# Reordering four kinds of helper work in a fused kernel: windowed attention and two feed-forward networks on one core

## The chip, the cores and the metric

The kernel runs on one core of one Trainium2 chip. A core has five engines with a queue each: TensorE (PE in the rows, its weight loads PEld), VectorE (DVE), ScalarE (ACT), GpSimd (POOL), and SyncE (SP), which here only issues transfers. Each engine works through its own instructions in the order in which they stand in its queue, and waits on semaphores for the others. The metric is the device time of one execution in microseconds (us), taken as the median of several executions; less is better.

## The reference

Attention over 4 batches, 8 heads, 576 positions and 64 channels, in which each query sees at most 32 keys (heads 0 to 3: the last 32 positions; heads 4 to 7: every fourth of the last 128); then two feed-forward networks of 2304 tokens, width 512, inner width 2048, one behind the other.

```python
scores = scale * np.matmul(q, k.transpose(0, 1, 3, 2))
scores = np.where(masks[None, :, :, :], scores, -1000000000.0)
attn = np.exp(scores - np.max(scores, axis=-1, keepdims=True))
attn_out = np.matmul(attn / (np.sum(attn, axis=-1, keepdims=True) + 1e-09), v)
x = np.ascontiguousarray(attn_out.transpose(0, 2, 1, 3)).reshape(B * S, H * D)
# network 1
h = x @ w_in
x = (np.maximum(h, 0.0) + alpha * np.minimum(h, 0.0)) @ w_out
# network 2
h = x @ w_in2
out = np.where(h >= 1, h, np.where(h <= -1, 0.0, (h + 1) ** 2 / 4.0)) @ w_out2
```

## The kernel before

**Split products.** Every large product is made of three matmuls in a reduced 32-bit format: each factor is split into a high part (a rounding copy on ACT, line 326) and a low part (source minus high part on POOL or DVE, line 327). For weights the parts are `wr` (of w_in) and `woh`, `wol` (of w_out); for the activations `xv` (input x) and `gh`, `gl` (the inner activation g). Lines 513 to 515 are the three matmuls of h = x w_in in the plain sub-tiles, lines 688 to 690 those of y = g w_out.

**Conversions.** The weights arrive as 64-bit words in staging tiles `st` (line 271, one transfer of 512 KB on SP's queue each) and are turned into 32-bit numbers by three DVE instructions: lines 320, 321 and 314. `conv(k)` issues the next k of these instructions. When the third is issued the staging tile is free and the next load is issued (`more`). Lists hold what is still to load (`pend_l`) and to convert (`pend_w`); the second network's 16 w_in tiles stand in `pend_2`. A conversion of the second network's w_in goes by `wf` to DRAM.

**Stages.** (1) Six attention groups alone. (2) The sub-tiles `PLAIN` = (0,0), (0,1), (0,2) of network 1, each in 16 slots f, one for every 128 inner columns; a counter k runs over the slots. A slot issues on PE the products h(f), an attention step and y(f-2); on the other engines the activation (`f_g`: line 650 on ACT, 653 on DVE, 660 on ACT for `gh`), the low part `gl` (`f_cut`, line 666), splits of weights and conversions. Twelve groups of attention run inside these slots, at the slots' two attention points: scores `s_ps` (line 148), their maximum and difference on DVE (155, 160), exp on ACT (164), a transpose on PE to `t_ps` (211), its copy to `pT` on ACT (213), the values' product `o_ps` (222), its scaling on DVE (228 to 230), a transpose to `x_ps` (237) and copies into x (255). (3) `PAIRS`, (0,3), (1,0) and (1,1): sub-tiles of 1024 tokens by a seven-product scheme (lines 544 to 546), whose combined inputs are sums made on DVE in PSUM (`room`, line 452) and then split into `xv`. Between two pairs stands a loop over `SECOND`, 16 steps of 12 matmuls each (the second half's y), in which the next pair's weights (`p_weights`) and inputs (`x_work`, 22 pieces of work, handed out by `more_x`) are prepared. (4) `LAST`.

**What sets the order.** The order on every engine is the order of the calls in the code; nothing is rescheduled. In slots 0 and 1 the products h(0) and h(1) have been issued already, so both slots run as fast as the other engines allow. `h_ps` has two PSUM tiles, so h(2) waits for line 653 of slot 0, which reads h(0). In network 1's first sub-tile `gl` is on POOL.

**The lines that the change touches.** `w_cut` splits the w_in tiles whose conversion is finished; `split_pending` splits the w_out tiles whose y is still to come; `EARLY` gives the number of conversion instructions in slots 0 and 1, `BEFORE` how many of a slot's stand between the parts of the activation.

Of the kernel before, what the change touches and what calls it, by code (L numbers as in the profile page):

```python
# [26 lines left out]
NF = DFF // P  # L27
# [29 lines left out]

FIRST = (0, 2)

EARLY = (3, 6)  # L60
READY = 12
BEFORE = ((1, 1), (1, 3))

# [4 lines left out]
PLAIN = ((0, 0), (0, 1), (0, 2))  # L68
# [19 lines left out]
def attention_then_two_ffns(ctx: ExitStack, tc: tile.TileContext, a0, aqk, av, w1i, w1o, w2i, w2o, alpha, masks, ident, out):  # L88
# [170 lines left out]
    wi, wo, wt, cv, cut = {}, {}, {}, {}, []  # L259
# [107 lines left out]
    def w_cut():  # L367
        while cut:
            w_split(*cut.pop(0))
# [335 lines left out]
    def pieces(ph):  # L705

        return [(ph, 0, 0), (ph, 1, 0)] + [x for f in range(NF) for x in ((ph, f + 2, 0), (ph, f, 1)) if x[1] < NF]
# [4 lines left out]
    with tc.manual_schedule(), ExitStack() as late:  # L712
# [19 lines left out]
        pend_l = pieces(0)  # L732
# [36 lines left out]
        def conv(k):  # L769

            for _ in range(k):
                if not todo and pend_w and pend_w[0] in cv:
                    todo.extend(w_make(*pend_w.pop(0)))
                if todo:
                    todo.pop(0)()
                    if not todo:
                        more()
# [47 lines left out]
        f_h(n0, 1, (2,))  # L825
        x_split(n0, 3)
        w_cut()
        conv(3)
        nc.vector.tensor_scalar(al, al, -1.0, 1.0, ALU.mult, ALU.add)
        a_load_qk(NGB + 1)  # L830
        a_load_v(NGB + 1)
# [45 lines left out]
        def more_x(k):  # L877
            for _ in range(min(k, len(x_work))):
                x_work.pop(0)()
# [7 lines left out]
        def split_pending():  # L887
            for x in pend_y:
                if x not in wos:
                    wo_split(*x)  # L890

        def one_y():
            f_y(*pend_y.pop(0))

        pend_2 = [(1, f, 0) for f in range(NF)]
        after_n = dict(zip(order, order[1:] + [None]))

        def slot(n, f, k):
            nn = after_n[n]
            if k != 1:  # L900
                split_pending()
            w_cut()
            if n == LAST and f == NF - 1:
                wo_split((n, 0), f)
            if k > 1 or n == LAST:
                f_h(n, f)
            early = f < 2 and k > 1
            if early:
                one_y()
            if n == PLAIN[0] and f == NF - 1:  # L910
                pend_l.extend(pend_2)
                pend_w.extend(pend_2)
            if n in PLAIN[:2] and f >= NF - NC:
                x_split(nn, f - NF + NC, n == PLAIN[1])
            if k in (0, 1):
                ops = EARLY[k]
            elif n == n0:
                ops = 6
            elif n != LAST:
                ops = 1 if n == PLAIN[1] else 3  # L920
            else:
                ops = 0
            attention_point()
            b0, b1 = BEFORE[n[0]]
            g = f_g(n, f, lambda: conv(min(ops, b0)))
            ops -= min(ops, b0)
            first_ops = min(ops, b1) if k else 1
            conv(first_ops)
            f_cut(n, f, g)
            if k == 0:  # L930
                wo_split((n, 0), f)
            w_cut()
            ahead = 2 if n == PLAIN[0] else 3
            for i in range(1, ahead + 1):
                if f + i < NF:
                    ready(n, f + i)
                elif nn and nn not in PAIRS:
                    ready(nn, f + i - NF)
            if n == PLAIN[2]:
                if f == 9:  # L940
                    turn = iter(range(1 << 30))
                    x_work.extend(x_seven(nn, lambda: ps_a.tile([P, TW], F32, tag="w" if nxt < NG or at else "wa"[next(turn) % 2], name="room")))
                if NF - 4 <= f < NF - 1:
                    p_weights(nn, 0, f - NF + 4)
                if f in (9, 10):
                    more_x(3)
                elif f >= READY:
                    more_x((5, 5, 6, len(x_work))[f - READY])
                if f == NF - 1:
                    p_weights(nn, 0, 3)  # L950
                if f == NF - 1:
                    r_free.extend(x_free[:2])
                    del x_free[:2]
            if n == LAST and f % 2 == 0 and 4 <= f // 2 + 3 < NF // 2:
                w_base(1, f // 2 + 3)
            if k >= 2 and not early:
                one_y()
            pend_y.append(((n, 0), f))
            attention_point()
            conv(ops - first_ops)  # L960
            more()

        k = 0
# [53 lines left out]
        for q, n in enumerate(PAIRS):  # L1017
# [41 lines left out]
            for i, f in enumerate(SECOND):  # L1059
                if i and loaded < NF:  # L1060
                    g_load(n, SECOND[loaded])
                    loaded += 1
                if 1 <= i < NF - 2:
                    wo_split((n, 1), SECOND[i + 2])
                if i == NF - 2:
                    more_x(len(x_work))
                    if nn in PAIRS:
                        step(q + 1, 0)
                    else:
                        pend_y += [((n, 1), x) for x in SECOND[i:]]  # L1070
                        break
                f_y((n, 1), f)
                more_x(2)
                if nn in PAIRS:
                    if i in (5, 13):
                        w_base(nn[0], i // 13)
                    if i == NF - 3:
                        r_free.extend(x_free[:2])
                        del x_free[:2]
                    elif i in (8, 9, 10, 11):  # L1080
                        p_weights(nn, 0, i - 8)
                else:
                    if i == 0:
                        r_free.extend(x_free[:8])
                        del x_free[:8]
                    if i % 4 == 0:
                        w_base(nn[0], i // 4)
                    elif i % 2 == 0:
                        ready(nn, i // 2 - 1)
                    if i % 4 == 0 and i:  # L1090
                        ready(nn, i // 2 - 1)
                if q == 0:
                    for _ in range((2, 1, 1, 0, 0, 1, 1, 1, 1)[i] if i < 9 else 0):
                        w_load(*pend_l.pop(0))
                    if i == 8:
                        spare += [0, 0]
                    if f in HELD:
                        wo[1, f] = w_pool(f).tile([P, DM], F32, tag=f"o{f}", name="wo")
                        nc.sync.dma_start(wo[1, f], whole[1, 1, f // 2][:, f % 2])
                    if i < NF - 1 and SECOND[i + 1] not in HELD:  # L1100
                        conv(3)
                    if i == NF - 4:
                        assert not pend_w and not todo and not cv
                        x_free.extend(st_free)
                        st_free.clear()
# [91 lines left out]
```

## Time and profile before

| what | value |
|---|---|
| median of 3 runs | 860.86 us (858.82 to 861.88) |
| the profiled execution: its time | 859.94 us |
| the profiled execution: span from first to last instruction | 858.2 us |
| mean granted clock of TensorE | 0.992 of 2.4 GHz |
| busy share of the span: PE, PEld, DVE, ACT, POOL | 98%, 80%, 65%, 50%, 56% |

The profiled execution lasts 1.7 us longer than its span, and it lies 0.92 us under the median. PE is the engine that sets the time, so a change of order can only win where PE stands still or runs at the lower clock. The rows further down are in the trace's form: start in us from the span's start, length in us, engine, line, operation, tile written <- tiles read, shapes, how many instructions the row holds, and in brackets the engine's idle time before the row with what ended it.

### The profile page before, as it was taken

The numbers are of one execution on the slowest core, as the hardware profiler recorded it, in microseconds if no ns is written. First come the engines' busy times: TensorE is split into PE (matmuls) and PEld (weight loads), VectorE is DVE, ScalarE is ACT, GpSimd is POOL, SyncE is SP. The second block draws the span as 40 slices with busy tenths as digits, with TensorE's granted clock in tenths as the row PEclk, the third lists the DMA queues.
The fourth block names the chain that finished last, engine by engine and source line by source line (L and its number), as shares of the span: only waits on it lengthen the run. The fifth ranks groups of instructions, "written<-read, shape, count | busy, mean of one in ns | idle before, by whom it ended". The sixth has DMA issues, their size and how long they took to land.

```text
span 858.2 us, 14266 instructions
## 1 busy us (share of the span) xinstructions
PE 837.3 (98%) x5328; PEld 688.7 (80%) x5330; DVE 554.5 (65%) x911; ACT 428.8 (50%) x803; POOL 481.9 (56%) x411
## 2 busy tenths in 40 slices
PE   6899999999999999999998999999999999999998
PEld 4677777998777778888886888888888888888898
DVE  4788786666877576776678677776418677640143
ACT  3444444665534565555444556464335545453365
POOL 2365545777444677767346676763662332346486
PEclk8899999999999999999999999999999999999999
DMA  7787653764661025444287735333935553548220
GB/s 298 236 245 224 198 166 113 223 216 124 194 187 50 1 74 179 141 152 167 99 330 270 275 131 203 141 156 112 344 123 188 201 195 126 173 139 302 70 79 25
DMA packets 54980, 147.45 MB, mean 172 GB/s; under 512 B 5632, under 2 KB 13440, under 8 KB 54912
## 3 DMA queue, kind: packets, MB, share of 16 engines
q1 hardware_dynamic: 54624, 146.39, 50.3%
q8 instruction: 42, 0.69, 0.3%
q14 instruction: 26, 0.21, 0.1%
q10 hardware_dynamic: 288, 0.16, 0.1%
HBM read 101.97 MB, written 44.56 MB: 171 GB/s over the span
## 4 chain that ended last, share of the span: by engine, by line
PE 88%; DVE 6%; ACT 2%; issue 2%; DMA 1%; POOL 1%; SPq 0%; ACTq 0%; DVEq 0%
PE y L688 14%; PE y L690 14%; PE y L689 14%; PE h_ps L546 9%; PE h_ps L544 9%; PE h_ps L545 9%; PE h_ps L513 5%; PE h_ps L515 4%; PE h_ps L514 4%; PE o_ps L222 2%; PE s_ps L148 1%; DVE room L452 1%; PE t_ps L211 1%; PE x_ps L237 1%; DVE w_ps L321 1%
## 5 line engine op out<-in xcount | busy, mean ns | idle before, releaser
L327 POOL TENSOR_TENSOR wol<-wo,woh 128x512 fp32r<-128x512 f32 x153 | 200.0, 1314 | 86.5 <-ACT woh L326 86.2
L688 PE MATMUL y<-gh,wol 128*128 128x512 f32 (+1 forms) x444 | 164.0, 369 | 0.6 <-POOL wol L327 0.6
L690 PE MATMUL y<-gl,woh 128*128 128x512 f32 (+1 forms) x444 | 160.2, 361 | 0.0
L689 PE MATMUL y<-gh,woh 128*128 128x512 f32 (+1 forms) x444 | 160.2, 361 | 0.0
L327 POOL TENSOR_TENSOR wr<-wb,wr 128x512 fp32r<-128x512 f32 x60 | 77.7, 1295 | 128.3 <-ACT wr L326 128.3
L546 PE MATMUL h_ps<-xv,wr 128*128 128x512 f32 x336 | 130.8, 389 | 0.0
L545 PE MATMUL h_ps<-xv,wr 128*128 128x512 f32 x336 | 130.8, 389 | 0.0
L544 PE MATMUL h_ps<-xv,wr 128*128 128x512 f32 x336 | 130.7, 389 | 0.0
L326 ACT ACTIVATE woh<-wo 128x512 fp32r<-128x512 f32 x153 | 93.6, 626 | 71.8 <-PE y L690 52.2
L327 POOL TENSOR_TENSOR wr<-wi,wr 128x512 fp32r<-128x512 f32 x50 | 64.5, 1290 | 98.4 <-ACT wr L326 98.2
L688 PEld LDWEIGHTS y<-gh,wol 128*128 128x128 f32 x444 | 83.7, 189 | 16.7 <-POOL wol L327 2.3
L513 PE MATMUL h_ps<-xv,wr 128*128 128x512 f32 (+1 forms) x256 | 90.7, 354 | 3.8 <-DVE g L653 2.0
L690 PEld LDWEIGHTS y<-gl,woh 128*128 128x128 f32 x444 | 83.6, 188 | 13.4
L689 PEld LDWEIGHTS y<-gh,woh 128*128 128x128 f32 x444 | 83.8, 189 | 12.2
L514 PE MATMUL h_ps<-xv,wr 128*128 128x512 f32 (+1 forms) x256 | 87.0, 340 | 0.2 <-DVE xv L327 0.2
L515 PE MATMUL h_ps<-xv,wr 128*128 128x512 f32 (+1 forms) x256 | 87.0, 340 | 0.0
L558 ACT ACTIVATE g<-g,half 128x512 f32<-128x512 f32 x64 | 44.7, 723 | 72.1 <-DVE g L557 70.9
L688 PE MATMUL y<-gx,wol 128*128 128x512 f32 x192 | 75.5, 393 | 2.7 <-POOL wol L327 2.7
L689 PE MATMUL y<-gx,woh 128*128 128x512 f32 x192 | 75.3, 392 | 0.0
L690 PE MATMUL y<-gx,woh 128*128 128x512 f32 x192 | 75.3, 392 | 0.0
L545 PEld LDWEIGHTS h_ps<-xv,wr 128*128 128x128 f32 x336 | 63.1, 188 | 13.2
L544 PEld LDWEIGHTS h_ps<-xv,wr 128*128 128x128 f32 x336 | 63.1, 188 | 13.2
(122 smaller groups left out, 1513.7 us busy)
## 6 DMA issues: line engine op xcount, KB each, us to landing
gd<-XA SPq DMA_DIRECT2D x42, 512.0 KB, 3.5
gx<-gd SPq DMA_DIRECT2D x42, 512.0 KB, 5.9
wb<-whole SPq DMA_DIRECT2D x30, 512.0 KB, 4.8
st<-w1i SPq DMA_DIRECT2D x16, 512.0 KB, 5.0
st<-w1o SPq DMA_DIRECT2D x16, 512.0 KB, 5.2
st<-w2i SPq DMA_DIRECT2D x16, 512.0 KB, 4.8
st<-w2o SPq DMA_DIRECT2D x16, 512.0 KB, 4.8
kept<-wr SPq DMA_DIRECT2D x16, 512.0 KB, 2.7
```

Source lines behind the costliest of these rows:

```text
L326: nc.scalar.activation(hi, src, AF.Copy)
L327: low_on.tensor_tensor(lo, src, hi.bitcast(F32), ALU.subtract)
L513: nc.tensor.matmul(ps[:, :w], r[:, 1, cs], x[:, 0, xs], start=(c == 0), stop=False)
L514: nc.tensor.matmul(ps[:, :w], r[:, 0, cs], x[:, 1, xs], start=False, stop=False)
L515: nc.tensor.matmul(ps[:, :w], r[:, 0, cs], x[:, 0, xs], start=False, stop=(c == NC - 1))
L544: nc.tensor.matmul(o, w[:, 1, cs], x[:, 0], start=start and m == 0, stop=False, skip_group_check=not start)
L545: nc.tensor.matmul(o, w[:, 0, cs], x[:, 1], start=False, stop=False, skip_group_check=not start)
L546: nc.tensor.matmul(o, w[:, 0, cs], x[:, 0], start=False, stop=m == 1, skip_group_check=not start)
L558: nc.scalar.activation(t, t, AF.Square, bias=half, scale=0.5)
L688: nc.tensor.matmul(o, wl[:, cs], gh[:, :w], start=(i == 0), stop=False)
L689: nc.tensor.matmul(o, wh[:, cs], gh[:, :w], start=False, stop=False)
L690: nc.tensor.matmul(o, wh[:, cs], gl[:, :w], start=False, stop=(i == NF - 1))
```

## The change

It moves work; the set of computing instructions is the same.

1. First conversions: ahead of slot 0 one conversion instruction is issued in place of three; slot 0 issues none between the parts of its activation and three behind it; `EARLY[0]` goes from 3 to 5, so the sum over both places stays at six.
2. Weight splits: in a slot, `w_cut` is called behind the activation and not ahead of the slot, unless the slot's own product lacks its weight; in slot 2 `split_pending` is called behind the first attention point.
3. Loads: `pend_2` goes into the list of loads in slot 13 of the first sub-tile, not in slot 15. The list of conversions gets it in slot 15 as before.
4. In the loop over `SECOND` between the first and the second pair (q = 0) `more_x` hands out three pieces of x's work in steps 0 to 2, one in steps 3 to 10 and three from step 11 on, in place of two in each. The loops of later pairs keep two.

```diff
-EARLY = (3, 6)
+EARLY = (5, 6)
...
         x_split(n0, 3)
         w_cut()
-        conv(3)
+        conv(1)
         nc.vector.tensor_scalar(al, al, -1.0, 1.0, ALU.mult, ALU.add)
...
         def slot(n, f, k):
             nn = after_n[n]
-            if k != 1:
+            if k not in (1, 2):
                 split_pending()
-            w_cut()
+            if k > 1 and (n, f) not in wt:
+                w_cut()
...
+            if n == PLAIN[0] and f == NF - 3:
+                pend_l.extend(pend_2)
             if n == PLAIN[0] and f == NF - 1:
-                pend_l.extend(pend_2)
                 pend_w.extend(pend_2)
...
             attention_point()
+            if k == 2:
+                split_pending()
             b0, b1 = BEFORE[n[0]]
-            g = f_g(n, f, lambda: conv(min(ops, b0)))
-            ops -= min(ops, b0)
-            first_ops = min(ops, b1) if k else 1
+            b0 = min(ops, b0) if k else 0
+            g = f_g(n, f, lambda: conv(b0))
+            ops -= b0
+            first_ops = min(ops, b1 if k else 3)
+            w_cut()
             conv(first_ops)
             f_cut(n, f, g)
             if k == 0:
                 wo_split((n, 0), f)
-            w_cut()
...
                 f_y((n, 1), f)
-                more_x(2)
+                more_x(2 if q else 1 if 3 <= i < 11 else 3)
```

PE's and POOL's instructions stand in the same order before and after. What moves stands on DVE, ACT and SP, at these places.

DVE, from the end of stage 1 into slot 0 (`wo` is the first w_out tile, `w_ps` a conversion's place in PSUM, line 653 slot 0's activation):

```order
 L320 TENSOR_SCALAR wo<-st 128x512
+L829 TENSOR_SCALAR al<-al 128x16
+L653 SCALAR_TENSOR_TENSOR g<-g,al,h_ps 128x512
 L321 SCALAR_TENSOR_TENSOR wo<-st,wo 128x512
 L314 SCALAR_TENSOR_TENSOR wo<-st,wo 128x512
-L829 TENSOR_SCALAR al<-al 128x16
-L320 TENSOR_SCALAR w_ps<-st 128x512
-L653 SCALAR_TENSOR_TENSOR g<-g,al,h_ps 128x512
-L321 SCALAR_TENSOR_TENSOR w_ps<-st,w_ps 128x512
+L320 TENSOR_SCALAR w_ps<-st 128x512
```

Slot 0's activation has moved ahead of three conversion instructions; behind slot 1's activation the two orders are the same up to slot 15.

ACT in slots 0 to 2, before:

```order
L660 ACTIVATE gh<-g 128x512
L326 ACTIVATE woh<-wo 128x512
L326 ACTIVATE wr<-wi 128x512
L164 ACTIVATE s<-s 128x384
L650 ACTIVATE g<-h_ps 128x512
L660 ACTIVATE gh<-g 128x512
L326 ACTIVATE woh<-wo 128x512
L326 ACTIVATE wr<-wi 128x512
L213 ACTIVATE pT<-t_ps 128x384
L650 ACTIVATE g<-h_ps 128x512
```

and in the change:

```order
L660 ACTIVATE gh<-g 128x512
L326 ACTIVATE woh<-wo 128x512
L164 ACTIVATE s<-s 128x384
L650 ACTIVATE g<-h_ps 128x512
L660 ACTIVATE gh<-g 128x512
L326 ACTIVATE wr<-wi 128x512
L213 ACTIVATE pT<-t_ps 128x384
L326 ACTIVATE woh<-wo 128x512
L650 ACTIVATE g<-h_ps 128x512
L660 ACTIVATE gh<-g 128x512
L326 ACTIVATE wr<-wi 128x512
```

The copy `pT` now has one split of a weight less ahead of it; in every later slot of the sub-tile the split of `wr` stands behind `gh`, so in each second slot it comes ahead of the exp of line 164 and no longer behind it.

SP around slots 13 to 15 (`qk`, `vz`: an attention group's queries and keys, and its values):

```order
 L123 DMA qk_86<-aqk 64x832
-L131 DMA vz_88<-av 64x3x260 x2
-L122 DMA qk_87<-aqk 64x832
-L123 DMA qk_87<-aqk 64x832
 L271 DMA st<-w2i 128x1024 x3
+L131 DMA vz_88<-av 64x3x260 x2
+L122 DMA qk_87<-aqk 64x832
+L123 DMA qk_87<-aqk 64x832
+L271 DMA st<-w2i 128x1024
```

The first three loads of the second network now stand ahead of one group's values and the next group's queries and keys. On DVE the six instructions of two conversions go from the third sub-tile to slot 15 and the slot behind it.

ACT in the second half of the loop over `SECOND` (`wr<-wb`, `wr<-ss`: the next pair's weights; `xv<-room`: splits of sums in PSUM), before:

```order
L326 ACTIVATE woh<-wo 128x512 x2
L326 ACTIVATE xv<-room 128x512 x2
L326 ACTIVATE wr<-wb 128x512
L326 ACTIVATE woh<-wo 128x512
L326 ACTIVATE xv<-room 128x512
L326 ACTIVATE wr<-ss 128x512
L326 ACTIVATE woh<-wo 128x512
```

and in the change:

```order
L326 ACTIVATE xv<-XA 128x512
L326 ACTIVATE woh<-wo 128x512
L326 ACTIVATE wr<-wb 128x512
L326 ACTIVATE woh<-wo 128x512
L326 ACTIVATE wr<-ss 128x512
L326 ACTIVATE woh<-wo 128x512
L326 ACTIVATE xv<-room 128x512
L326 ACTIVATE wr<-ss 128x512
```

The splits of the next pair's first two weights have no split of a sum ahead of them any more.

## Rows read from the trace of the kernel before

**Rows 1.** The page, part 1: busy us, share of the span, instructions.
```profile
PE 837.3 (98%) x5328; PEld 688.7 (80%) x5330; DVE 554.5 (65%) x911; ACT 428.8 (50%) x803; POOL 481.9 (56%) x411
```

**Rows 2.** Windows of 20 us: length, busy us by engine, granted clock, DMA share, GB/s.
```profile
40.00:60.00 20.00, 18.55 (x123) 14.37 (x122) 17.65 (x30) 9.51 (x18) 14.01 (x11) 0.92 0.93 266
...
140.00:160.00 20.00, 18.30 (x163) 16.25 (x163) 11.41 (x23) 10.60 (x25) 12.01 (x10) 1.00 0.61 187
...
260.00:280.00 20.00, 18.60 (x139) 14.13 (x141) 15.64 (x23) 9.99 (x21) 9.77 (x7) 1.00 0.13 53
...
460.00:480.00 20.00, 17.30 (x74) 13.55 (x74) 11.46 (x18) 6.75 (x12) 16.44 (x17) 1.00 0.61 189
```

**Rows 3.** Timeline, end of stage 1 and slots 0 to 2.
```profile
35.13 1.52 DVE L320 TENSOR_SCALAR wo<-st 128x512 int32<-128x512 int32 x1
...
36.04 0.60 ACT L650 ACTIVATE g<-h_ps 128x512 f32<-128x512 f32 x1 [1.03 <-PE h_ps L515]
...
38.70 0.74 DVE L653 SCALAR_TENSOR_TENSOR g<-g,al,h_ps 128x512 f32<-128x512 f32 x1
...
39.58 0.53 PE L513 MATMUL h_ps<-xv,wr 128*128 128x512 f32 x1 [1.95 <-DVE g L653]
...
43.28 0.75 DVE L653 SCALAR_TENSOR_TENSOR g<-g,al,h_ps 128x512 f32<-128x512 f32 x1 [0.86 <-ACT g L650]
...
47.63 0.63 ACT L326 ACTIVATE wr<-wi 128x512 fp32r<-128x512 f32 x1 [1.61 <-DVE wi L314]
...
48.69 0.87 PE L222 MATMUL o_ps<-vz,pT 128*32 128x130 f32 x24 [1.46 <-ACT pT L213]
...
49.16 0.75 DVE L653 SCALAR_TENSOR_TENSOR g<-g,al,h_ps 128x512 f32<-128x512 f32 x1 [0.90 <-ACT g L650]
```

**Rows 4.** Timeline, slots 3 and 4: activation, exp and transpose of the second group.
```profile
55.74 0.74 DVE L653 SCALAR_TENSOR_TENSOR g<-g,al,h_ps 128x512 f32<-128x512 f32 x1
...
57.69 0.53 ACT L164 ACTIVATE s<-s 128x384 f32<-128x384 f32 x1
...
59.36 0.49 PE L211 MATMUL t_ps<-idt,s 128*128 128x128 f32 x3
```

**Rows 5.** Windows, one microsecond behind the first wait.
```profile
40.00:41.00 1.00, 1.00 (x4) 0.81 (x3) 0.96 (x3) 0.62 (x2) 0.82 (x1) 0.50 1.00 390
```

**Rows 6.** Timeline, change from the first to the second sub-tile.
```profile
140.36 1.48 SPq L271 DMA_DIRECT2D st<-w2i  x3
...
144.87 0.39 ACT L650 ACTIVATE g<-h_ps 128x256 f32<-128x256 f32 x1
...
146.57 0.69 DVE L320 TENSOR_SCALAR w_ps<-st 128x512 int32<-128x512 int32 x1 [4.93 <-DMA st<-w2i]
...
147.18 0.48 DVE L653 SCALAR_TENSOR_TENSOR h_ps<-g,al,h_ps 128x256 f32<-128x256 f32 x1
...
149.99 0.39 PE L513 MATMUL h_ps<-xv,wr 128*128 128x256 f32 x1 [1.70 <-POOL wr L327]
```

**Rows 7.** Timeline, third sub-tile.
```profile
267.32 0.68 DVE L314 SCALAR_TENSOR_TENSOR wf<-st,w_ps 128x512 int32<-128x512 int32 x1
...
272.35 0.55 PE L237 MATMUL x_ps<-idt,o 128*128 128x128 f32 x3 [0.55 <-DVE s L152]
```

**Rows 8.** Timeline, loop over `SECOND` between the first and the second pair.
```profile
457.66 1.09 ACT L326 ACTIVATE xv<-room 128x512 fp32r<-128x512 f32 x2 [2.69 <-DVE room L452]
...
459.35 1.30 POOL L327 TENSOR_TENSOR wr<-wb,wr 128x512 fp32r<-128x512 f32 x1 [3.01 <-ACT wr L326]
...
463.49 1.26 POOL L327 TENSOR_TENSOR wol<-wo,woh 128x512 fp32r<-128x512 f32 x1
...
464.81 0.50 PE L688 MATMUL y<-gx,wol 128*128 128x512 f32 x1 [2.30 <-POOL wol L327]
...
471.06 0.50 PE L688 MATMUL y<-gx,wol 128*128 128x512 f32 x1 [0.40 <-POOL wol L327]
```

**Rows 9.** Line 452 in the first 480 us: ns least/median/most.
```profile
L452 DVE TENSOR_TENSOR room<-XA x8: 729/1452/1802, 268.7 to 455.2; 128x512 f32<-128x512 f32 x8
```

## The prediction

> **What bounds the kernel now.** I read the page first. TensorE is busy for 98% of the span, every other engine for at most 65% of it (its weight loads apart) [rows 1]. The change leaves TensorE's and GpSimd's order as it is and adds no instruction, so it can only give back time in which TensorE stands still (858.2 - 837.3 = 20.9 us in all) or runs at half clock. The second view is the table of windows: four of them, each with one of the change's places in it, show TensorE below 20 us of 20, by 1.45, 1.70, 1.40 and 2.70 us [rows 2]; that is 7.25 us, and to it comes what half clock costs in the first. The third view is the timeline at these places, to see what TensorE waits for there and how much of the wait its cause can be rid of.
>
> **First conversions and splits, slots 0 to 4.** The reader is to see this chain [rows 3]: ACT has slot 0's g ready at 36.04 + 0.60 = 36.64, but DVE runs three more conversion instructions and reaches line 653 only at 38.70; it ends at 39.44, and h(2), which needs its PSUM tile, starts at 39.58 after 1.95 us of idle. Just behind it the granted clock is 0.50, TensorE's 1.2 GHz [rows 5]. The second wait is 1.46 us, for `pT`, which stands on ACT behind a weight split that itself sat idle for a conversion until 47.63.
>
> In the new order line 653 follows the conversion instruction that ends at 35.13 + 1.52 = 36.65, so with its 0.74 us h(2) can start at about 37.6. The copy `pT` loses the split ahead of it. Seen from TensorE alone that would give back 1.95 + 1.46 us and what h(2) loses at half clock, well over 3.4 us. I do not take that, because DVE is the engine that is full here: 17.65 us of 20 [rows 2]. Up to line 653 of slot 3, which ran at 55.74 [rows 4], DVE has the same instructions before and after. The only time that it can save is its idle time in front of the activations of slots 1 and 2, 0.86 + 0.90 = 1.76 us [rows 3]: it reaches 54.0. From there the chain is as before: from 55.74 to the end of the exp, 57.69 + 0.53 = 58.22, took 2.48 us, and one more split now stands on ACT ahead of the exp, about 0.55 us as ACT spaces them (0.63 long [rows 3], overlapping a little). So the transpose `t_ps`, at 59.36 before [rows 4], can start at 54.0 + 2.48 + 0.55, about 57.1. TensorE could be there earlier and waits: I expect a new wait for the exp at `t_ps` of 1 to 2 us. The gain at this place is then 59.36 - 57.1 = 2.3 us.
>
> Against this edit speaks contention of DVE and GpSimd. A sum of two SBUF tiles took between 0.73 and 1.80 us [rows 9], so up to 1.07 us more for the same work. The first w_out tile's third conversion instruction also reads two SBUF tiles (`st` and `wo`), and now stands beside GpSimd's `gl` of slot 0. If it loses that race the gain is 2.3 - 1.1 = 1.2 us. Both would start near 38.2: the one when line 653 (to 37.4) and one more conversion instruction of 0.7 us are done, the other when `gh`, 0.6 us behind line 653, is. So I take 1.8, between the two; the ends are 0 (below, first rival) and 2.9 (if the split ahead of the exp is covered too). The Trainium skill (SBUF — State Buffer, section "SBUF: two separate sides") states the rule behind it: VectorE with two SBUF inputs and GpSimd take a shared port pair as a lock for a whole instruction, and the loser is blocked fully. By that rule the loss is all or nothing, so the gain would be 2.3 or 1.2 and never between; the rows here show both ends and cannot tell which one falls to this place.
>
> **The earlier loads.** DVE sat idle for 4.93 us in front of the first conversion of the second network, whose load was issued at 140.36; the next activation, line 653, was queued behind that conversion and ran at 147.18, although ACT had delivered its input at 144.87 + 0.39 = 145.26; from there the way led to the split of a weight on GpSimd and to TensorE's wait of 1.70 us at 149.99 [rows 6]. With the loads two slots earlier (a slot is some 6.6 us: 49.16 to 55.74 [rows 3, 4]; load to first use was 6.2 us) the data is there. Six conversion instructions move into this idle time, 6 x 0.69 = 4.1 us of 4.93. Line 653 can start at about 145.3, 1.9 us earlier, so all of the 1.70 goes. I take 1.6; the low end is 0.9, if the filled DVE delays line 653 by one conversion, 0.69. What else moves: three loads now stand in SP's queue ahead of one group's values and the next group's queries. They wait for staging tiles that conversions of slots 13 to 15 set free, so they hold up the queue by less than two slots, and both groups are needed later than that. I cost it at nothing.
>
> **The slots that lose these conversions.** In the third sub-tile six conversion instructions fall away on DVE. At 272.35 TensorE waits 0.55 us for DVE's line 152, with one such instruction 5 us ahead of it at 267.32 [rows 7]; two of them gone between the activation and line 152 are 1.4 us. I take 0.6, that wait and a little; ends 0 and the window's 1.40 [rows 2].
>
> **x's sums respaced.** POOL sits idle for 3.01 us until ACT splits `wr` for the next pair; ACT has two splits of sums ahead of it, and these wait 2.69 us for DVE's sum in PSUM. POOL then runs without a pause into the `wol` that TensorE waits for: 2.30 us, and once more 0.40 [rows 8]. In the new order no split of a sum stands ahead of the first two weight splits, so POOL can start up to 3.01 us earlier, which is more than 2.30. POOL's chain from there to the `wol` at 463.49 and its end at 464.75 is full; 3.01 us earlier it ends at 461.7, and TensorE wants it at 464.81 - 2.30 = 462.5. So both waits go: 2.7 us. The margin of 0.8 us is thinner than one more contention of 1.07 us [rows 9], so I take 2.6, with ends of 1.6 (two such) and 2.7. The work that moves: the sums of the last part are made at steps 8 to 12 in place of 7 to 10. They are wanted by the pair's products, which start behind step 13, a step or more later; I cost that at nothing, and without that cover it would be the length of a late sum, 0.7 us or more, within the low end.
>
> **The sum.** 1.8 + 1.6 + 0.6 + 2.6 = 6.6 us. Against the profiled execution's own time, 859.94 us (its span 858.2 and 1.7 around it), that is 853.3 us; against the median of the runs, 860.86, which is 0.9 higher, it would be 854.3. I give 853.3. The ends of the four terms add up to 2.5 and 8.6 us, so 851.3 to 857.4 us; with the 0.9 between execution and median and as much on the other side, 850.5 to 858.3.
>
> **The rivals.**
>
> *The first place gives nothing.* DVE stays late by all it saved, for instance because the lost race of [rows 9] happens twice: 4.8 us remain, 855.1 us. For it speaks DVE's 88% [rows 2]; against it that its idle of 1.76 us is in the rows. Chance 0.15.
>
> *The wait at the respaced sums only moves.* GpSimd's chain is full from 459.35 on, and if its first split stays late through a released tile and not through ACT's order, the 2.30 stays and 4.0 us remain: 855.9 us. Against it: the row names ACT as releaser [rows 8]. Chance 0.12.
>
> *Nothing to measure.* Each shortened wait turns up at the next engine within a slot, and the gain stays within 0.3% (2.6 us, about what a measurement of this kernel can tell from no change): some 859 us. Chance 0.08.
>
> *Slower: the split ahead of the exp.* In each second slot of the first sub-tile one more weight split now stands on ACT ahead of the exp, and `t_ps` waits for the exp. Before, the exp ended at 58.22 and TensorE reached `t_ps` at 59.36, 1.1 us of room [rows 4]; 0.55 of it are left. As long as DVE delivers line 653 as early as before, relative to TensorE, this costs nothing. If DVE does not make up its lateness of the first slots, the wait that I expect once, up to 1.9 us, comes back in all six further groups of the sub-tile: 6 x 1.9 = 11.4 us, less 6.6, which is 4.8 us slower: 864.7 us. It decides from 6.6 / 6 = 1.1 us for each group on. Against it: no work is added to DVE in these slots. Chance 0.07.
>
> **How the numbers follow.** My forecast has 0.58 and the time of 853.3 us. The two rivals at 855 and 856 lie in the range. 850.5 to 858.3 leaves out the last two rivals, 0.15, and little on the lower side. Faster by over 0.3% are the forecast and the first two rivals, 0.85, of which I take 0.02 off for a median that falls high: 0.83. Within 0.3%: 0.10. Slower: 0.07.
>
> **What would show it.** Right: h(2) starts near 37.6 with no wait, the granted clock is not halved around 40 us, and `t_ps` of the second group has a wait of 1 to 2 us for the exp near 57; DVE has no idle for a load of the second network near 145 and TensorE no wait at the first h of the second sub-tile; no `wol` wait over 0.5 us in the loop between the pairs, with POOL's first `wr` right behind a `wol`. Wrong: waits at `t_ps` in the slots between 60 and 140 us, a late values' load behind the three loads, or DVE at work on sums when the pair's first products want them.

## The result and the profile after

The changed kernel takes 852.0 us (median of 6 runs, 851.1 to 853.0), the kernel before on the same chip 860.9 (6 runs, 858.8 to 861.9). The ratio is 0.9904, with a 95% interval of 0.9888 to 0.9919: 8.3 us less, 7.0 to 9.6. The forecast was 853.3, with a range of 850.5 to 858.3. The profiled execution of the changed kernel took 853.0 us, with a span of 851.2.

The page's span and first part, to be read against [rows 1]:

```profile
span 851.2 us, 14291 instructions
PE 835.7 (98%) x5330; PEld 687.2 (81%) x5330; DVE 556.0 (65%) x911; ACT 428.6 (50%) x803; POOL 483.4 (57%) x411
```

TensorE's time outside its busy time went from 20.9 us to 15.5; its busy time itself is 1.6 us less, where the half clock of [rows 5] is gone. The windows of [rows 2] in the changed kernel:

```profile
40.00:60.00 20.00, 18.07 (x124) 13.35 (x123) 19.35 (x33) 9.96 (x19) 12.92 (x11) 1.00 1.05 264
140.00:160.00 20.00, 19.99 (x200) 18.16 (x198) 13.79 (x27) 13.48 (x31) 13.48 (x11) 1.00 0.70 229
260.00:280.00 20.00, 19.22 (x146) 14.56 (x145) 12.38 (x19) 10.27 (x20) 10.18 (x8) 1.00 0.00 1
460.00:480.00 20.00, 20.00 (x89) 16.42 (x89) 14.87 (x22) 9.32 (x17) 14.89 (x13) 1.00 0.67 235
```

Two places are clean now. At 40 us TensorE still stands for 1.9 us, but at full clock, and DVE is busy for 19.35 of 20 us. In the third window the wait at 272 us is gone, and another, of 0.75 us at 275, is left. The waits of TensorE behind stage 1, by cause:

```profile
PE o_ps L222 <- ACT pT L213: 1.1, 2, 0.8
PE s_ps L141 <- DVE o L230: 0.8, 1, 0.8
PE y L688 <- POOL wol L327: 0.6, 1, 0.6
PE t_ps L211 <- ACT s L164: 0.5, 1, 0.5
```

The timeline at the change's places, to be read against [rows 3, 4, 6, 7, 8]:

```profile
36.83 0.60 ACT L650 ACTIVATE g<-h_ps 128x512 f32<-128x512 f32 x1 [1.02 <-PE h_ps L515]
37.66 0.75 DVE L653 SCALAR_TENSOR_TENSOR g<-g,al,h_ps 128x512 f32<-128x512 f32 x1
38.55 0.47 PE L513 MATMUL h_ps<-xv,wr 128*128 128x512 f32 x1
39.04 0.69 DVE L314 SCALAR_TENSOR_TENSOR wo<-st,wo 128x512 int32<-128x512 int32 x1
39.15 1.75 POOL L666 TENSOR_TENSOR gl<-g,gh 128x512 fp32r<-128x512 f32 x1 [1.97 <-DMA st<-w1o]
...
42.00 0.55 PE L211 MATMUL t_ps<-idt,s 128*128 128x128 f32 x3 [0.48 <-ACT s L164]
45.70 0.87 PE L222 MATMUL o_ps<-vz,pT 128*32 128x130 f32 x24 [0.39 <-ACT pT L213]
50.52 0.35 PE L141 MATMUL s_ps<-mask,idt 128*32 128x384 bf16 x4 [0.81 <-DVE o L230]
54.81 0.74 DVE L653 SCALAR_TENSOR_TENSOR g<-g,al,h_ps 128x512 f32<-128x512 f32 x1
57.28 0.54 ACT L164 ACTIVATE s<-s 128x384 f32<-128x384 f32 x1
57.87 0.31 PEld L211 LDWEIGHTS t_ps<-idt,s 128*128 128x128 f32 x3 [0.56 <-ACT s L164]
57.88 0.55 PE L211 MATMUL t_ps<-idt,s 128*128 128x128 f32 x3
...
143.59 0.49 DVE L653 SCALAR_TENSOR_TENSOR h_ps<-g,al,h_ps 128x256 f32<-128x256 f32 x1 [0.46 <-ACT g L650]
146.44 0.39 PE L513 MATMUL h_ps<-xv,wr 128*128 128x256 f32 x1
268.31 0.55 PE L237 MATMUL x_ps<-idt,o 128*128 128x128 f32 x3
275.47 0.87 PE L222 MATMUL o_ps<-vz,pT 128*32 128x130 f32 x24 [0.75 <-ACT pT L213]
457.19 1.30 POOL L327 TENSOR_TENSOR wol<-wo,woh 128x512 fp32r<-128x512 f32 x1
458.61 0.43 PE L688 MATMUL y<-gx,wol 128*128 128x512 f32 x1
464.22 0.39 PE L688 MATMUL y<-gx,wol 128*128 128x512 f32 x1
```

The first row is a landmark: ACT's `g` of slot 0 comes ahead of every edit and ran at 36.04 before [rows 3]. So this execution was 0.79 us later when the change began, and what each place gave is read from the distance to it.

| Start of | before | after | change | gained since the row above |
|---|---|---|---|---|
| slot 0's `g` (ACT) | 36.04 | 36.83 | +0.79 | |
| second `t_ps` of the sub-tile | 59.36 | 57.88 | -1.48 | 2.27 |
| first `h` of the second sub-tile | 149.99 | 146.44 | -3.55 | 2.07 |
| `x_ps` of the third sub-tile | 272.35 | 268.31 | -4.04 | 0.49 |
| first `y` that waited for `wol` | 464.81 | 458.61 | -6.20 | 2.16 |
| second such `y` | 471.06 | 464.22 | -6.84 | 0.64 |

Together 7.63 us. The difference of the two spans, 7.0, is smaller by most of the 0.79, and the medians differ by more, since the profiled execution of before lay 1.0 us below its median and this one 1.0 above its own.

### The profile page after: what moved, and what is told of

Read it like the earlier page. It is cut to its first block, busy times and chain, and to the rows that moved or that the text cites. A ratio compares the mean times of both kernels' runs of the same rounds, so it can differ in the third digit from the quotient of the medians.

```text
span 851.2 us, 14291 instructions
## 1 busy us (share of the span) xinstructions
PE 835.7 (98%) x5330; PEld 687.2 (81%) x5330; DVE 556.0 (65%) x911; ACT 428.6 (50%) x803; POOL 483.4 (57%) x411
## 4 chain that ended last, share of the span: by engine, by line
PE 81%; DVE 7%; DMA 5%; ACT 3%; issue 2%; POOL 1%; SPq 0%; ACTq 0%; DVEq 0%; POOLq 0%
PE y L688 14%; PE y L690 14%; PE y L689 14%; PE h_ps L544 7%; PE h_ps L545 7%; PE h_ps L546 7%; PE h_ps L513 5%; PE h_ps L515 4%; PE h_ps L514 4%; DMA gd<-XA 3%; PE o_ps L222 2%; PE s_ps L148 1%; ACT wr L326 1%; PE t_ps L211 1%; DVE w_ps L320 1%
```

## The experiments

Every kernel was timed against the kernel before on its chip. The first four take one part of the change each. For slots 0 to 4 a measure is used that no chance in stage 1 disturbs: the time from slot 0's `g` to the second `t_ps`, 59.36 - 36.04 = 23.32 us before and 57.88 - 36.83 = 21.05 after. It repeats from run to run: 23.30 and 23.33 us in the two runs that leave this place as it was before (the loads alone, x's sums alone), 21.03 in the last run of this section, which leaves it as it is in the change.

**The conversions alone (e1_conv_only).**

```diff
-EARLY = (3, 6)
+EARLY = (5, 6)
...
-        conv(3)
+        conv(1)
...
-            g = f_g(n, f, lambda: conv(min(ops, b0)))
-            ops -= min(ops, b0)
-            first_ops = min(ops, b1) if k else 1
+            b0 = min(ops, b0) if k else 0
+            g = f_g(n, f, lambda: conv(b0))
+            ops -= b0
+            first_ops = min(ops, b1 if k else 3)
```

> The kernel before with the first edit alone: the first conversions stand behind line 653, the weight splits stay where they were. Theory A (VectorE is the full engine at this place, and only its idle time of 0.86 + 0.90 us can be given back): h(2) starts near 37.6 without a wait and TensorE is not at half clock behind it, but the split of slot 1 still stands on ACT ahead of pT and still waits for a conversion, so o_ps stays near 48 us and VectorE keeps most of its 0.90 us of idle time; at line 653 of slot 3 it is at most 0.9 us earlier. Time 0 to 0.9 us less than before. Theory B (TensorE's waits add up): 1.95 us of wait and about 1.6 us of half clock go, 3 to 3.6 us less than before.

860.35 us against 860.51, ratio 1.0003 (0.9994 to 1.0012): nothing. From `g` to the second `t_ps` it takes 59.46 - 35.97 = 23.49 us. Its timeline (DVE, ACT and PE):

```profile
37.67 0.47 PE L513 MATMUL h_ps<-xv,wr 128*128 128x512 f32 x1
41.87 0.63 ACT L326 ACTIVATE wr<-wi 128x512 fp32r<-128x512 f32 x1 [2.35 <-DVE wi L314]
42.40 0.51 ACT L164 ACTIVATE s<-s 128x384 f32<-128x384 f32 x1
42.96 0.84 PE L211 MATMUL t_ps<-idt,s 128*128 128x128 f32 x3 [2.29 <-ACT s L164]
43.42 0.75 DVE L653 SCALAR_TENSOR_TENSOR g<-g,al,h_ps 128x512 f32<-128x512 f32 x1 [0.86 <-ACT g L650]
44.02 0.63 PE L689 MATMUL y<-gh,woh 128*128 128x512 f32 x1
48.83 0.87 PE L222 MATMUL o_ps<-vz,pT 128*32 128x130 f32 x24 [0.96 <-ACT pT L213]
49.30 0.75 DVE L653 SCALAR_TENSOR_TENSOR g<-g,al,h_ps 128x512 f32<-128x512 f32 x1 [0.90 <-ACT g L650]
```

`h(2)` starts at once, at full clock, and TensorE is up to 3.5 us ahead of before at 43.3 us. Then it waits 2.29 us for the exp, which stands on ACT behind a weight split that waits for a conversion, and the matmuls behind that wait take 0.63 us in place of 0.39, half clock (the granted clock is 0.51 from 43 to 46 us). At `o_ps` all is given back. DVE's idle times of 0.86 and 0.90 are those of [rows 3], unchanged. Theory B falls.

**The weight splits alone (e2_split_only).**

```diff
-            if k != 1:
+            if k not in (1, 2):
                 split_pending()
-            w_cut()
+            if k > 1 and (n, f) not in wt:
+                w_cut()
...
+            if k == 2:
+                split_pending()
...
+            w_cut()
             conv(first_ops)
             f_cut(n, f, g)
...
-            w_cut()
```

> The kernel before with the second edit alone: the weight splits stand behind the copies of transposes, the conversions stay ahead of line 653. Theory A (VectorE is full here): line 653 of slot 0 stays at 38.7 and h(2) at 39.6, pT comes up to 1 us earlier, VectorE's 0.90 us of idle time goes; 0.9 to 1.5 us less than before. Together with the first edit 1.8 to 2.3. Theory B (waits add up): the 1.46 us of o_ps go whole, and with the first edit's 3 to 3.6 that is 5. Rival (the split ahead of the exp): t_ps waits for the exp in the second slots of all groups of the first sub-tile, 5 us slower than before.

857.35 us, ratio 0.9965 (0.9952 to 0.9978), 3.0 us less. Its timeline in slots 0 to 4 and at 143 and 462 us:

```profile
39.82 0.47 PE L513 MATMUL h_ps<-xv,wr 128*128 128x512 f32 x1 [1.94 <-DVE g L653]
42.57 0.74 DVE L653 SCALAR_TENSOR_TENSOR g<-g,al,h_ps 128x512 f32<-128x512 f32 x1
47.45 0.74 DVE L653 SCALAR_TENSOR_TENSOR g<-g,al,h_ps 128x512 f32<-128x512 f32 x1
58.06 0.49 PE L211 MATMUL t_ps<-idt,s 128*128 128x128 f32 x3
...
143.96 0.70 DVE L320 TENSOR_SCALAR w_ps<-st 128x512 int32<-128x512 int32 x1 [3.57 <-DMA st<-w2i]
...
462.33 0.50 PE L688 MATMUL y<-gx,wol 128*128 128x512 f32 x1 [2.42 <-POOL wol L327]
464.41 0.63 PE L689 MATMUL y<-gx,woh 128*128 128x512 f32 x1
```

TensorE's largest wait and the half clock behind it are still there, yet both idle times of DVE are gone, and `g` to `t_ps` takes 58.06 - 36.29 = 21.77 us, 1.55 less. Theory A's reason holds, but it is this edit alone that frees DVE. The run is faster than Theory A said. In its trace DVE idles 3.57 us for the second network's load and not 4.93, and TensorE's wait at the first `h` of the second sub-tile is 0.7 us and not 1.7. Most of this can't be put down to the edit: the load came into use 5.2 us after its issue, before 6.2, and in the runs of the first and of the fourth edit alone, whose code is the same there as before, the load took 5.7 us and TensorE waited 1.14 and 1.22. Beyond the 1.55 us, what the 3.0 consist of stays open.

**The earlier loads alone (e3_loads_only).**

```diff
+            if n == PLAIN[0] and f == NF - 3:
+                pend_l.extend(pend_2)
             if n == PLAIN[0] and f == NF - 1:
-                pend_l.extend(pend_2)
                 pend_w.extend(pend_2)
```

> The kernel before with the second network's first loads queued two slots earlier, nothing else. Theory A (terms 1.6 for the loads and 0.6 for the third sub-tile): VectorE's 4.93 us of idle time at 145 us is filled, TensorE's 1.70 us at 150 us go, the 0.55 us at 272 us go; 2.2 us less than before, up to 2.5. Theory B (the wait comes back when the staging tiles run out in the third sub-tile, or late values hold up the next group): 1.6 us or less.

858.69 us, ratio 0.9986 (0.9978 to 0.9995): 1.2 us less, half of the 2.2. In the trace both waits are gone: the `h` of 149.99 starts at 148.39, the `x_ps` of 272.35 at 270.26, 2.1 us earlier. In this execution some is lost again at 463 us. There TensorE waits 2.43 us for `wol`, and the matmuls behind that wait run at half clock; in the kernel before they did not, after a wait of 2.30 us [rows 8]. The lead shrinks to 0.6 us by 468 and is 1.3 at the end.

**x's sums alone (e4_sums_only).**

```diff
-                more_x(2)
+                more_x(2 if q else 1 if 3 <= i < 11 else 3)
```

> The kernel before with x's sums respaced, nothing else. Theory A (ACT's queue of sums is what holds GpSimd): GpSimd has no 3.01 us of idle time at 459 us, both waits for wol go (2.30 and 0.40 us), 2.6 to 3.0 us less than before. Theory B (the wait only moves along GpSimd's full chain, or to the sums that now come later): 0 to 0.5 us less than before.

856.59 us, ratio 0.9958 (0.9945 to 0.9971), 3.6 us less. The `y` of 464.81 starts at 462.05, that of 471.06 at 467.62, neither with a wait; 2.76 and 3.44 us earlier, of which 0.30 were there at 150 us already. Theory A holds.

**All but the first edit, all but the second (e5_all_but_conv, e6_all_but_split).** The diffs are those of e1 and e2 backwards, on the changed kernel.

> The changed kernel with the first edit undone (conversions ahead of line 653 again). From the two single runs: the second edit alone brought 1.3 us at the first place, both together 2.3, so the first edit is worth 1.0 us in the company of the second though it was worth nothing alone. Theory A (VectorE's idle time is what there is to win, and it takes both edits to reach the second half of it): 1.0 us more than the changed kernel, 853. Rival (the first edit is worth nothing, since TensorE's wait only moves): the changed kernel's time, 852. Rival (TensorE's 1.95 us and the half clock behind it come back whole): 3 us more, 855.

> The changed kernel with the second edit undone (weight splits ahead of the copies again). Theory A: as in the run of the first edit alone, TensorE gains 3.5 us up to 43 us and gives them back in a wait of 2.3 us for the exp and the half clock behind it; 2.3 us more than the changed kernel, 854.3. At 150 us nothing further, since the earlier loads have taken that wait away already. Rival (the second edit has a worth of its own at 150 us, as the 1.1 us there in its single run suggest): 3.4 us more, 855.4.

Without the first edit: 851.88 us against 859.88, ratio 0.9901 (0.9885 to 0.9916), the changed kernel's own. From `g` to `t_ps` it takes 57.92 - 36.14 = 21.78 us, 0.73 more than with it. So the trace gives this edit 0.7 us in the company of the second, less than the two ratios, each with an interval of 2.7 us, can tell. Without the second edit: 854.1 us, ratio 0.9933 (0.992 to 0.9945), some 2.5 us more than the changed kernel; `g` to `t_ps` takes 59.20 - 35.70 = 23.50, as in the first run, with a wait of 2.31 us for the exp. Nothing further is lost at 150 us. So of the 2.27 us the second edit brings 1.55 by itself, and the first nothing by itself and 0.73 in its company. Where the 0.73 come from is in the trace without the first edit: the exp has ended there at 56.88, 1.04 us ahead of `t_ps`. With DVE's idle time gone TensorE, after its wait of 1.94 us and the half clock behind it, is the later of the two, and this is what the first edit takes away.

**Two conversion instructions later (e7_less_early, e8_less_early_and_third).**

```diff
-EARLY = (5, 6)
+EARLY = (5, 4)
```

and in the second of them also

```diff
-                if f in (9, 10):
+                if f == 9:
                     more_x(3)
...
-                    more_x((5, 5, 6, len(x_work))[f - READY])
+                    more_x((5, 2, 6, len(x_work))[f - READY])
...
             attention_point()
+            if n == PLAIN[2] and f == 10:
+                more_x(3)
```

> The changed kernel with four conversion instructions in place of six in slot 1, the two others later. Theory A (at 50 us TensorE's wait of 0.81 us for line 230 is VectorE's backlog of conversions, 19.35 us busy of 20): two instructions less, 1.4 us, ahead of line 230; the wait goes and 0.8 us are won, 851.2. Rival (the weights that come 1.4 us later are then waited for at h or y): no gain, or up to 1 us more than the changed kernel.

> The run before it, and in the third sub-tile the variants of x made elsewhere: in slot 10 behind the copy of the transposes and not ahead of it (TensorE waits 0.75 us for that copy at 275 us), in slots 13 to 15 two, six and the rest in place of five and six (GpSimd has two splits of x ahead of the wol that TensorE waits for at 299 us, 0.58 us). Theory A (each of these waits is only an order): 0.8 + 0.75 + 0.6 = 2.1 us less than the changed kernel, 849.9. Rival (the work moved to the last slots is late for the pair's first products at 305 to 310 us): the 0.6 or more come back there, 850.5 to 851.5.

874.71 us, ratio 1.0164 (1.0149 to 1.0178), and 873.47, ratio 1.016: both some 14 us slower than the kernel before, and far outside what I had expected. The wait of 0.81 us at `s_ps` did go. TensorE's first row of waits in the former, and its timeline around one `h`:

```profile
PE h_ps L513 <- POOL wr L327: 17.9, 12, 3.0
```

```profile
62.16 0.75 DVE L653 SCALAR_TENSOR_TENSOR g<-g,al,h_ps 128x512 f32<-128x512 f32 x1 [4.35 <-ACT g L650]
62.82 0.68 DVE L314 SCALAR_TENSOR_TENSOR wi<-st,w_ps 128x512 int32<-128x512 int32 x1
63.48 0.61 ACT L326 ACTIVATE wr<-wi 128x512 fp32r<-128x512 f32 x1
64.17 1.26 POOL L327 TENSOR_TENSOR wr<-wi,wr 128x512 fp32r<-128x512 f32 x1 [5.57 <-ACT wr L326]
65.49 0.50 PE L513 MATMUL h_ps<-xv,wr 128*128 128x512 f32 x1 [0.82 <-POOL wr L327]
```

The third instruction of each w_in tile now stands behind the activation of line 653, and its split with it. So a ring closes in every slot: the activation waits for the `h` of this slot, the weight of the next `h` for the activation, that `h` for the weight. Six instructions a slot are just what a slot needs, so the two are never made up, and 12 slots pay. In the third sub-tile the second kernel won the 0.75 and 0.58 us of its two places (the distance to the changed kernel shrinks from 22.2 us to 20.65 at 299 us) and lost them right behind, where TensorE waits 0.3 and 1.1 us for sums and splits that now come in the last slots.

**The normalisation ahead, and one more split of x earlier (e9_norm_first, e11_norm_first_and_third).**

```diff
-EARLY = (5, 6)
+EARLY = (5, 4)
...
-                ops = 6
+                ops = 8 if k == 2 else 6
...
-            w_cut()
+            if k != 2:
+                w_cut()
             conv(first_ops)
+            if k == 2:
+                w_cut()
```

and in the second of them slot 10 as above, and

```diff
-                    more_x((5, 5, 6, len(x_work))[f - READY])
+                    more_x((7, 4, 5, len(x_work))[f - READY])
```

> The changed kernel with lines 228 to 230 ahead of two conversion instructions in VectorE's order and not behind them; slot 1 makes four instructions and slot 2 eight, and the weight split of slot 2 stands behind its conversion, so that no weight is split a slot later, as in the run that lost 22 us. Theory A (that run was slow because the split of each weight slid behind the next activation, and the wait for line 230 is an order of VectorE's): the wait of 0.81 us goes, no wait for wr comes, 0.5 to 0.9 us less than the changed kernel's 852.0. Rival (any two conversion instructions made later cost the slots behind them): 5 to 22 us more.

> The run before it, and in the third sub-tile the variants of x of slot 10 behind the copy of the transposes (0.75 us of wait at 275 us), and those of slots 12 to 14 as seven, four and five in place of five, five and six, so that GpSimd has one split of x less ahead of the wol of slot 13 (0.58 us of wait at 299 us) and none comes later than before. Theory A (waits of order): 0.8 + 0.75 + 0.6 = 2.1 us less than the changed kernel, 849.9. Rival (GpSimd's split now in slot 12 is late there, or VectorE's sums are late at 304 us, as the 1.1 us in the other spacing): the 0.6 or more come back, 850.5 to 851.5.

851.69 us, ratio 0.99 (0.9885 to 0.9915): the same as the changed kernel, so the ring was the cause of the 22 us. But the 0.8 us are not won:

```profile
48.20 0.35 PE L141 MATMUL s_ps<-mask,idt 128*32 128x384 bf16 x4
52.98 0.52 PE L237 MATMUL x_ps<-idt,o 128*128 128x128 f32 x3 [0.84 <-DVE s L160]
56.40 0.55 PE L211 MATMUL t_ps<-idt,s 128*128 128x128 f32 x3
```

The wait stands at `x_ps` now, 0.84 us for DVE's line 160, and from `g` to `t_ps` it is 56.40 - 35.37 = 21.03 us. My Theory A, a wait of order, falls here: with DVE busy for 18.96 us of 20, this order only picked another place at which TensorE waits for it. The other kernel took 854.22 us, ratio 0.9934 (0.9921 to 0.9946): slot 10 gave its 0.8 us, but GpSimd's split in slot 12 waited for ACT until 291.88 and kept `wol` behind it, on which TensorE waited 2.42 us at 294.4.

**A lost race (e12_lost_race).**

```diff
+    idle = const.tile([P, 128], F32, name="idle")
...
-            conv(first_ops)
+            if k:
+                conv(first_ops)
+            else:
+                conv(1)
+                nc.vector.memset(idle, 0.0)
+                nc.vector.memset(idle, 0.0)
+                conv(first_ops - 1)
```

> The changed kernel with two short memsets of a tile that nobody reads on VectorE ahead of line 314 of the first w_out tile in slot 0, so that GpSimd's gl of slot 0 starts first (in the changed kernel line 314 started 0.11 us ahead of it, took 0.69 us, and gl took 1.75 in place of 1.29). By the lock of the whole instruction: line 314 takes 1.5 to 1.8 us and ends about 0.6 us behind gl, gl takes 1.29; VectorE, the full engine there, is 1.1 to 1.4 us later, and t_ps of the second group with it: 1.1 to 1.4 us more than the changed kernel, 853.3. By a shared port (both slower while they overlap): line 314 takes about 1.0, and 0.5 us more, 852.5.

The lines behind the new tile's are one higher, line 314 is 315 here:

```profile
37.32 1.30 POOL L667 TENSOR_TENSOR gl<-g,gh 128x512 fp32r<-128x512 f32 x1 [1.97 <-ACT gh L661]
37.49 1.67 DVE L315 SCALAR_TENSOR_TENSOR wo<-st,wo 128x512 int32<-128x512 int32 x1
41.43 0.55 PE L212 MATMUL t_ps<-idt,s 128*128 128x128 f32 x3 [1.74 <-ACT s L165]
57.29 0.55 PE L212 MATMUL t_ps<-idt,s 128*128 128x128 f32 x3
```

GpSimd was first by 0.17 us, and the conversion took 1.67 us and ended 0.54 us behind `gl` (38.62 to 39.16); in the changed kernel DVE was first by 0.11, and it was `gl` that grew, from 1.30 to 1.75, and ended 1.17 behind line 314 (39.73 to 40.90). From `g` to the second `t_ps` it takes 57.29 - 35.00 = 22.29 us, 1.24 more; by the times 852.91 us, ratio 0.9914 (0.99 to 0.9927), 0.9 more, not surely told from the changed kernel. Not all of the 1.24 is the race: DVE gets to the conversion 2.49 us after `g`, in the changed kernel 2.21, and these 0.28 us go to the two memsets. The blocked instruction costs 1.67 - 0.69 = 0.98, close to the 1.1 of the prediction, and both ends of its price are now seen at the place itself. The rival, a conversion of about 1.0 us because both go on more slowly, is not what the row shows. The Trainium skill (SBUF — State Buffer, section "SBUF: two separate sides") has it that whichever of the two starts first keeps the port pair for its whole instruction; the rows agree both ways round.

**Three orders of the third sub-tile (e13_third_reordered).**

```diff
-                own(6, m),
                 plain(4, 1, 0, m),
                 plain(5, 1, 1, m),
             ]
+            ops.insert(len(ops) - (0 if m and n == PAIRS[0] else 2), own(6, m))
...
-                if f in (9, 10):
+                if f == 9:
                     more_x(3)
                 elif f >= READY:
-                    more_x((5, 5, 6, len(x_work))[f - READY])
+                    if f == READY + 1:
+                        more_x(1)
+                        wo_split((n, 0), f)
+                    more_x((5, 4, 6, len(x_work))[f - READY])
...
             attention_point()
+            if n == PLAIN[2] and f == 10:
+                more_x(3)
```

> The changed kernel with three orders of the third sub-tile changed: the variants of x of slot 10 behind the copy of the transposes (0.75 us of TensorE's wait at 275 us), the w_out split of slot 13 ahead of two splits of x on GpSimd (0.58 us at 299 us), and in slot 14 the split of a sum behind the two plain splits, so that the next activation does not stand behind a split that waits for that sum. Theory A (waits of order): 1.3 us less than the changed kernel's 852.0, 850.7, ratio to before 0.988. Rival (at 305.6 us TensorE starts 0.08 us behind the low part of the last activation, so what is won at 299 us comes back there): the 0.75 alone, 851.3, ratio 0.989. Below: no gain at all, if VectorE's sums of slots 12 to 14, not TensorE, set the time of these activations, 852.

849.68 us (849.5 to 850.0), ratio 0.9881 (0.9864 to 0.9897), 10.2 us less than the kernel before and some 2 less than the changed one, with overlapping intervals of the ratios. Its windows from 260 us on:

```profile
260.00:280.00 20.00, 19.97 (x149) 15.47 (x150) 12.29 (x19) 10.30 (x20) 10.88 (x9) 1.00 0.00 1
280.00:300.00 20.00, 20.00 (x91) 16.56 (x90) 13.60 (x19) 12.41 (x24) 14.43 (x13) 1.00 0.00 1
300.00:320.00 20.00, 20.00 (x90) 16.58 (x89) 15.68 (x24) 12.58 (x24) 15.12 (x15) 1.00 0.41 132
```

Neither of the waits at 275 and 299 us is left, and none comes behind them. From slot 0's `g` to the end the trace is 2.2 us shorter than the changed kernel's: 0.8 at 275 us and 0.8 at 299 are these orders'. Some 0.4 lie near 394 us, where the changed kernel's profiled execution waited 0.16 us for a conversion; the runs without the first edit, with the normalisation ahead and with the lost race have no such wait either, so that is not the gain of an order. Here DVE is busy for 12 to 16 us of 20: where the engine has room, an order was worth what it removed.

## Why the prediction was right

**The first place** was forecast at 1.8 us and gave 2.27. The working held in its core: DVE is the full engine, TensorE's 1.95 us and the half clock behind it are not what can be won, and the forecast start of `h(2)`, 37.6, is 38.55 - 0.79 = 37.8. The chain behind it came out link by link: line 653 of slot 3 at 54.81 - 0.79 = 54.0, as forecast, the end of the exp 57.28 + 0.54 - 54.81 = 3.01 us after it (2.48 + 0.55 in the sum), and `t_ps` 0.06 us behind the exp. The sum by TensorE's waits, well over 3.4 us, is refuted by the first run, which removes the wait of 1.95 us and the half clock behind it and gains nothing. What the term mis-sized is the race: I took 1.8 between 2.3 and 1.2, and this kernel wins it by 0.11 us; losing it costs 0.98. So 1.8 was a value that neither outcome could give, and that the better one came is luck. Two things were wrong without harm. I gave the gain to both edits for DVE's idle time, and the splits alone free all of that; what the first edit adds, 0.73, is TensorE's own lateness, which I had put at nothing. And the new wait of 1 to 2 us for the exp did not show as idle time of TensorE at the second `t_ps`: DVE's lateness had cost it 0.48, 0.39 and 0.81 us at `t_ps`, `o_ps` and `s_ps` ahead of it, 1.68 together, because the normalisation of lines 228 to 230 waits in the same queue; I had followed that queue from activation to activation only.

**The earlier loads**: 1.6 forecast, 2.07 between the two landmarks; TensorE's 1.70 are gone whole and line 653 waits for ACT alone, 0.46 us. But 0.2 of the 2.07 come at 125 us and belong to the second edit (the two runs with it and without the first have them, the runs of the loads alone and without the second have not). And the 1.70 is at the long end of what the kernel before does there: 1.14 and 1.22 in the two runs with the same code at this place, so about 0.5 of the gain is the chance of the execution that I read. SP's queue cost nothing, as costed. **The third sub-tile**: 0.6 forecast, 0.49 measured. A loss of 0.3 us near 394 us, with a wait of 0.16 for a conversion of the second network, was not forecast; five other runs with the earlier loads (the loads alone, those without the first and without the second edit, with the normalisation ahead, with the lost race) have no such wait, so the loads do not bring it and it is that execution's.

**x's sums**: 2.6 forecast; 2.16 + 0.64 and the 0.3 lost on the way, 3.1, and 3.1 in the single run. All of it went, and a wait costs more than the idle time in its row: in the first run the two `y` matmuls around the 2.42 us stand 464.46 - 461.65 = 2.81 us apart, where 0.23 is the step without one, so 2.58. The margin that I put at 0.8 us is 0.12: GpSimd's `wol` ends at 458.49 and TensorE takes it at 458.61. GpSimd's line 403 took 1.19 us ahead of it, 0.74 before; one more such loss there would have shown.

**The sum**: 2.27 + 2.07 + 0.49 - 0.3 + 3.1 = 7.6 in the traces, and 8.3 (7.0 to 9.6) by the times, against 6.6: the gain was taken too low. That 853.3 came within 1.3 us of 852.0 is in part luck: the 6.6 are taken from the profiled execution's 859.94, and from the median of 860.9 they would have given 854.3, 2.3 us off.

**The rivals.** The first place gives nothing: that is the run of the first edit alone, and not the change, which gained 2.27 us there. Nothing to measure: no, the interval of the ratio ends at 0.9919. The respaced wait only moves: no, GpSimd's idle 3.01 us were ACT's order, as the row said. The split ahead of the exp: no wait at any `t_ps` between 57.88 and 140 us; in the four groups behind 57.88 the exp still ends 1.1 to 1.4 us ahead of `t_ps`, before 1.4 to 1.7.

## What to carry to other kernels

Ask of a wait whether the engine that it waits for has idle time in the slots around: here the idle time of DVE was worth 1.55 us by itself, and TensorE's wait of 1.95 us, taken away by itself, nothing. Where DVE was busy for some 19 of 20 us, another order only moved TensorE's wait (0.81 us at `s_ps` became 0.84 at `x_ps`); where it was busy for 12 to 16, the waits that an order caused could be had whole, though only at the third try: the two orders before it lost again a few slots on what they had won. Before two instructions are moved later, look whether another engine's work is cut off behind them: a weight split that slid behind the next activation cost 22 us where 0.8 were looked for.

## What was unexpected in the hardware

A blocked instruction of DVE or GpSimd shows no idle time in its row. It shows as a long instruction: 1.67 us for 0.69, 1.75 for 1.30. A line's mean hides it; the spread of durations tells.

The same wait does not always cost TensorE its clock. Behind 2.42 us of idle time at the `wol` of the pairs' loop the granted clock stayed full in the run of the conversions alone (1.00 from 460 to 480 us), and fell to half in the run of the splits alone (0.91 over the same window, with matmuls of 0.63 us in place of 0.39 up to 467 us); behind 2.30 us in the kernel before it stayed full. What decides it is not in these runs. It costs about 1 us here at the end: the profiled executions of the splits alone and of the loads alone paid it, and that of the whole change, which has no wait there, did not, so the four single gains need not add up to the whole.
